# A half slot for the fifteenth expert slot of a top-1 mixture of experts

## The chip, the cores and the metric

The kernel runs on one core of a Trainium2 chip. The metric is device time in microseconds (us) of one execution, as the median of several runs. TensorE multiplies (PE in the views, PEld its weight loads), VectorE (DVE), ScalarE (ACT) and GpSimd (POOL) work element by element, and SyncE (SP) issues most of the transfers. PE writes into PSUM, from where ACT and DVE take the results.

## The reference, cut to what matters

```python
attn = sigmoid(q @ k.T / sqrt(64) - log(448)) @ v      # 4 batches, 12 heads, 448 tokens, heads of 64
x    = attn as (1792 tokens, 768)
e    = argmax(x @ w_gate, axis=1)                      # 8 experts, one per token
g    = softmax(x @ w_gate)[token, e]
x    = g * (relu(x @ w1[e]) @ w2[e])                   # w1: 768 x 1024, w2: 1024 x 768
h    = relu(x @ w_in)                                  # 768 x 2048
out  = (h * h) @ w_out                                 # 2048 x 768
```

With the inputs of the reference, worked out from its code, the eight experts get 25, 19, 434, 5, 260, 235, 456 and 358 tokens.

## The kernel before, in words

The kernel has three stages: attention with the gate's logits, the experts, and the two dense layers at the end. Its order is written out by hand; each engine takes its instructions in that order, and so does each queue of transfers.

**Numbers in two parts.** A product of two f32 numbers is made from parts that TensorE takes at a faster rate: a high part (ACT copies it, f32 to f32r) and a low part (DVE subtracts the high part from the number). `split_w` does both for a chunk of weights. A product then needs three passes over the weights: high by high, low by high, high by low. `passes` issues them.

**Slots.** A slot is 128 rows of one expert. The rows of a slot are gathered from `x_d` by an indirect transfer (`gather`), transposed and split (`xtrans`), multiplied by w1 in four chunks (`up(c)`, c = 0 to 3, three passes of three matmuls over 512 columns each), transposed (`htrans`), multiplied by w2 in four chunks (`down(c)`, c = 4 to 7, three passes of four matmuls over 384 columns each), scaled by the gate (`fin`) and written to `y_d`. Slots 0 and 1 take rows of the expert with the most tokens among the first twelve blocks of tokens, before all tokens are routed. The other slots are laid out over the experts in order. While slot s runs, the weights of slot s+1 are split chunk by chunk (`next_chunk`, `split_m`) and those of slot s+2 are loaded; a slot from the third on loads only if its expert differs from that of the slot before (`regd`).

**Quarter slots.** The last rows of an expert, if they are 1 to 32, go to one of four quarter slots, which use f32 weights directly and run a piece at a time between the chunks of slots 3 to 12. Their rows are copied to their place in `y_d` at the end of the first layer (`quarter_rows`).

**How many.** `NTL + 1` = 15 slots always run. Further ones stand in a conditional block (`tc.If(more < NT)`), which runs only if the rows need it. With the tokens above, slots 0 and 1 take 256 rows of expert 6, four experts use a quarter slot, and the rest needs 13 slots: 15 in all. Expert 2, with 434 tokens, takes four of them, the last one with 50 rows.

**Routing on DVE.** `slots` works out how many rows each expert gets in slots, `late_places` the place of each token, `late_picks` and `spots` the one-hot tables from which TensorE picks the rows of the slots (`pick_rows`, line 227). `slots` comes in slot 0 after the second chunk, `late_places` and the tables at the end of slot 0, `pick_rows` in slot 1 between the second and third chunk. `quarters` works out the quarter slots in slot 2, and `gates` after it fills the gate table `gts`, which ACT needs for the first result of slot 2 (`fin(6)`).

**The last slot.** In slot 14 no weights of a further slot are split. Between its chunks 0 to 3 the first four tiles of `y_d` are transposed for the dense layers (`trans_y`, line 721). Each uses the two PSUM tiles px0 and px1, which ACT (line 726) and DVE (line 727) empty. After chunks 4 and 5 the first weights of the dense layers are split (`stage`). Then comes the conditional block (line 1071) and the first dense layer (`layer1`, lines 1245 to 1247).

## Time and profile before

| | before |
|---|---|
| median of 3 runs | 929.45 us (929.14 to 930.36) |
| the profiled execution | 928.85 us |
| its span | 927.4 us |
| PE busy | 917.4 us (99%) |
| PEld busy | 771.8 us (83%) |
| DVE busy | 692.6 us (75%) |
| ACT busy | 567.5 us (61%) |
| POOL busy | 101.0 us (11%) |
| mean granted clock | 0.998 |

The span is the part of the profiled execution that the hardware recorded; 1.45 us of its time lie around it. The time of an instruction runs from its start to its modelled end, and matmuls overlap: what a row of matmuls costs is read from the starts of the rows that follow it, not from its length.

### The profile page before, as it was taken

The numbers are of one execution on the slowest core, as the hardware profiler recorded it, in microseconds if no ns is written. First come the engines' busy times: TensorE is split into PE (matmuls) and PEld (weight loads), VectorE is DVE, ScalarE is ACT, GpSimd is POOL, SyncE is SP. The second block draws the span as 40 slices with busy tenths as digits, with TensorE's granted clock in tenths as the row PEclk, the third lists the DMA queues.
The fourth block names the chain that finished last, engine by engine and source line by source line (L and its number), as shares of the span: only waits on it lengthen the run. The fifth ranks groups of instructions, "written<-read, shape, count | busy, mean of one in ns | idle before, by whom it ended". The sixth has DMA issues, their size and how long they took to land. (4 is left out here: it accounts for less than half of the span.)

```text
span 927.4 us, 15244 instructions
## 1 busy us (share of the span) xinstructions
PE 917.4 (99%) x5803; PEld 771.8 (83%) x5803; DVE 692.6 (75%) x849; ACT 567.5 (61%) x711; POOL 101.0 (11%) x139
## 2 busy tenths in 40 slices
PE   9999999999999999999999999999999999999997
PEld 4555555589888888889998888889999999999997
DVE  3888886599887776877866998748878766569863
ACT  5767665768777867767764455455544466666541
POOL 1000001110411110101001222110000210000002
PEclk9999999999999999999999999999999999999999
DMA  8798977672687969693445988564333355456312
GB/s 297 262 369 323 335 230 243 239 290 73 245 290 280 354 242 360 238 403 138 164 183 187 364 298 287 193 237 154 100 105 119 125 179 174 140 177 238 127 35 102
DMA packets 63986, 206.37 MB, mean 223 GB/s; under 512 B 9330, under 2 KB 29138, under 8 KB 62754
## 3 DMA queue, kind: packets, MB, share of 16 engines
q1 hardware_dynamic: 43570, 159.85, 49.4%
q0 software_dynamic: 9040, 39.73, 11.2%
q10 hardware_dynamic: 11296, 5.75, 2.2%
q8 instruction: 47, 0.77, 0.3%
q14 instruction: 33, 0.27, 0.1%
HBM read 210.40 MB, written 45.63 MB: 276 GB/s over the span
## 5 line engine op out<-in xcount | busy, mean ns | idle before, releaser
L501 DVE TENSOR_TENSOR wl<-raw,wh 128x1536 fp32r<-128x1536 f32 x109 | 190.0, 1758 | 55.1 <-ACT wh L500 51.9
L500 ACT ACTIVATE wh<-raw 128x1536 fp32r<-128x1536 f32 x109 | 160.0, 1482 | 0.4 <-ACT xn L444 0.4
L398 ACT ACTIVATE a<-sc,bias_s 128x896 f32<-128x896 f32 x96 | 82.6, 912 | 55.0 <-PE sc L394 55.0
L1426 PE MATMUL pq<-wrh,sh 128*128 128x384 f32 x264 | 89.0, 337 | 0.0
L1428 PE MATMUL pq<-wrh,sl 128*128 128x384 f32 x264 | 88.8, 336 | 0.0
L1427 PE MATMUL pq<-wrl,sh 128*128 128x384 f32 x264 | 88.7, 336 | 0.0
L501 DVE TENSOR_TENSOR wrl<-raw,wrh 128x1536 fp32r<-128x1536 f32 x25 | 43.8, 1756 | 22.3 <-ACT wrh L500 21.6
L500 ACT ACTIVATE wrh<-raw 128x1536 fp32r<-128x1536 f32 x25 | 37.0, 1483 | 38.1 <-PE pq L1428 38.1
L404 PE MATMUL po<-a,qkv 128*64 128x448 f32 x288 | 59.6, 548 | 0.0
L764 PE MATMUL py<-wh,hh 128*128 128x384 f32 x240 | 55.4, 352 | 0.0
L1272 DVE TENSOR_TENSOR sl<-h,sh 128x1024 fp32r<-128x1024 f32 (+1 forms) x47 | 51.6, 1111 | 4.2 <-ACT sh L1271 4.2
L764 PE MATMUL ph<-wh,xh 128*128 128x512 f32 x180 | 53.4, 405 | 0.0
L764 PE MATMUL ph<-wl,xh 128*128 128x512 f32 x180 | 52.9, 402 | 0.0
L764 PE MATMUL py<-wh,hl 128*128 128x384 f32 x240 | 51.8, 337 | 0.0
L764 PE MATMUL ph<-wh,xl 128*128 128x512 f32 x180 | 51.6, 395 | 0.0
L764 PE MATMUL py<-wl,hh 128*128 128x384 f32 x240 | 51.6, 336 | 0.0
L1428 PEld LDWEIGHTS pq<-wrh,sl 128*128 128x128 f32 x264 | 49.5, 188 | 0.3 <-DVE sl L1272 0.3
L1427 PEld LDWEIGHTS pq<-wrl,sh 128*128 128x128 f32 x264 | 49.5, 188 | 0.0
L1426 PEld LDWEIGHTS pq<-wrh,sh 128*128 128x128 f32 x264 | 49.5, 188 | 0.0
L1271 ACT ACTIVATE sh<-h 128x1024 fp32r<-128x1024 f32 (+1 forms) x47 | 44.5, 962 | 7.6 <-PE pq L1427 6.7
L404 PEld LDWEIGHTS po<-a,qkv 128*64 128x64 f32 x288 | 18.4, 136 | 32.7 <-issue 30.0
L1251 ACT ACTIVATE r<-pp 128x512 f32<-128x512 f32 x32 | 19.1, 598 | 43.0 <-PE pp L1247 42.9
(447 smaller groups left out, 2156.9 us busy)
## 6 DMA issues: line engine op xcount, KB each, us to landing
raw<-in_wm SPq DMA_DIRECT2D x110, 768.0 KB
qraw<-in_wm SPq DMA_DIRECT2D x32, 768.0 KB
raw<-t_d SPq DMA_DIRECT2D x28, 768.0 KB
cs<-in_w SPq DMA_DIRECT2D x9, 1536.0 KB
qkv<-in_qk SPq DMA_DIRECT2D x23, 480.0 KB
whc<-in_w SPq DMA_DIRECT2D x14, 768.0 KB
qkv<-in_v SPq DMA_DIRECT2D x24, 256.0 KB
w_d<-cd POOLq DMA_DIRECT2D x8, 768.0 KB, 8.3
```

Source lines behind the costliest of these rows:

```text
L398: nc.scalar.activation(a[:, :n], ps[:, :n, :S], AF.Sigmoid, bias=bias_s, scale=1.0 / math.sqrt(D))
L404: nc.tensor.matmul(po[64 * h:64 * h + 64, :S], vr[:, 128 * c + 64 * h:128 * c + 64 * h + 64], a[:, h], start=(c == 0), stop=False, skip_gr ...
L500: nc.scalar.activation(h, src, AF.Copy)
L501: nc.vector.tensor_tensor(l, src, f32(h), op=ALU.subtract)
L764: nc.tensor.matmul(ps, left(i, q), right(j, q), start=first and a == 0 and q == 0, stop=last and a == 2 and q == n - 1)
L1251: nc.scalar.activation(r[:, :N], pp[:, :N], AF.Relu)
L1271: nc.scalar.activation(sh[:, :2 * N], src, AF.Copy)
L1272: V.tensor_tensor(sl[:, :2 * N], src, f32(sh[:, :2 * N]), op=ALU.subtract)
L1426: nc.tensor.matmul(po[p][:, :DH], lh, wc[:, w0:w0 + DH], start=(q == 0 and kk == 0 and o in (0, 2, 5)), stop=False, **fl)
L1427: nc.tensor.matmul(po[p][:, :DH], lh, wcl[:, w0:w0 + DH], start=False, stop=False, **fl)
L1428: nc.tensor.matmul(po[p][:, :DH], ll, wc[:, w0:w0 + DH], start=False, stop=(q == 3 and kk == 1), **fl)
```

## The change

The base has 14 slots and a half slot. One expert whose last rows are 33 to 64 gives them to the half slot (the first such expert; here expert 2 with its 50 rows). The half slot gathers 64 rows; `xtrans` puts their high parts into columns 0 to 63 and their low parts into columns 64 to 127 of one operand. `up` and `down` of `make_half` run two passes over each chunk (the operand by the high weights, by the low weights). The result has 128 rows: rows 0 to 63 from the high parts, rows 64 to 127 from the low parts; the two belong together. For the hidden layer the sum is made by the transposition: instead of a transposition against the identity, `htrans` multiplies by `fold`, two identities of 64 below one another, in f32, and the ReLU comes after it. The final 128 rows go to `yh_d`; in the first dense layer they are read back as two tiles of 64 rows (`half_rows`), added on DVE and written to their place in `y_d` ahead of the quarter rows. The weights of the half slot are loaded in any case. The conditional block begins one slot earlier.

Routing gets more work: six more DVE instructions in `slots`, two more in `late_places`, eight more in `quarters`, and tables of 25 instead of 24 columns. `gates` issues two more transfers on POOL.

```diff
-LC = LSLOT + NQ
+LC = LSLOT + 1 + NQ
+HM = 64
+QC = NSLOT + 1
+NMAIN = NTL
-NBASE = NTL + 1
+NBASE = NMAIN + 1
...
+    fold = const.tile([128, HM], F32, name="fold")
+    nc.gpsimd.tensor_tensor(fold, ident[:, :HM], ident[:, HM:], op=ALU.add)
...
         V.tensor_tensor(sa[:, 0, 1:], full, t30, op=ALU.add)
+        V.tensor_scalar(t30, pn, 63.5 - HM, TWO30, op0=ALU.add, op1=ALU.add)
+        V.scalar_tensor_tensor(half, t30, -TWO30, full, op0=ALU.add, op1=ALU.subtract)
+        V.tensor_tensor(half, half, cand, op=ALU.subtract)
+        V.tensor_tensor_scan(hs, seg[:, 0, 1:E + 1], half, 0.0, op0=ALU.mult, op1=ALU.add)
+        V.scalar_tensor_tensor(half, hs, -128.0, half, op0=ALU.is_ge, op1=ALU.mult)
+        V.tensor_tensor(sa[:, 0, 1:], sa[:, 0, 1:], half, op=ALU.add)
...
-        V.scalar_tensor_tensor(dlt, qs[:, :E], -128.0 * LSLOT, sx[:, 0, 1:], op0=ALU.add, op1=ALU.add)
+        V.scalar_tensor_tensor(dlt, half, 0.0, qs[:, :E], op0=ALU.is_equal, op1=ALU.mult)
+        V.scalar_tensor_tensor(dlt, dlt, -128.0 * (LSLOT + 1), sx[:, 0, 1:], op0=ALU.add, op1=ALU.add)
+        V.tensor_tensor(dlt, dlt, half, op=ALU.subtract)
...
-                nc.tensor.transpose(pt[:, j - j0, :], xg[:, j * 128:(j + 1) * 128], ident)
-            nc.scalar.activation(xh[:, j0:j0 + n], pt[:, :n], AF.Copy)
-            nc.vector.tensor_tensor(xl[:, j0:j0 + n], pt[:, :n], f32(xh[:, j0:j0 + n]), op=ALU.subtract)
+                nc.tensor.transpose(pt[:, j - j0, :w], xg[:w, j * 128:(j + 1) * 128], ident[:w, :w])
+            nc.scalar.activation(xh[:, j0:j0 + n, :w], pt[:, :n, :w], AF.Copy)
+            low = xl[:, j0:j0 + n] if w == 128 else xh[:, j0:j0 + n, w:]
+            nc.vector.tensor_tensor(low, pt[:, :n, :w], f32(xh[:, j0:j0 + n, :w]), op=ALU.subtract)
...
+        def make_half(s, xc):
...
+            def htrans(i):
+                pt = ps_ht.tile([128, 4, 128], F32, tag="pht", name=f"pht_{s}_{i}")
+                for f in range(4):
+                    nc.tensor.matmul(pt[:, f, :HM], hr[i][:, f * 128:(f + 1) * 128], fold, start=True, stop=True, skip_group_check=True)
+                hi, lo = (hc[:, 4 * i:4 * i + 4, HM * k:HM * k + HM] for k in range(2))
+                nc.scalar.activation(hi, pt[:, :, :HM], AF.Relu)
+                nc.vector.scalar_tensor_tensor(lo, pt[:, :, :HM], 0.0, f32(hi), op0=ALU.max, op1=ALU.subtract)
+
+            def both(out, first, last, steps, left, right, turn=None):
+                for a in range(2):
+                    for q in range(steps):
+                        nc.tensor.matmul(out, left(q), right(a, q), start=first and a == 0 and q == 0,
+                                         stop=last and a == 1 and q == steps - 1)
+                    if a == 0 and turn:
+                        turn()
+
+            def up(c):
+                i = c // 2
+                if c % 2 == 0:
+                    ps[i] = ps_h.tile([128, 512], F32, tag=f"ph{i}", name=f"ph_{s}_{i}")
+                both(ps[i], c % 2 == 0, c % 2 == 1, 3, lambda q: xc[:, 3 * (c % 2) + q, :],
+                     lambda a, q: (mh[c], ml[c])[a][:, q * 512:q * 512 + 512], (lambda: htrans(0)) if c == 2 else None)
+                if c % 2 == 1:
+                    hr[i] = mp.tile([128, 512], F32, tag="hr", name=f"hr_{s}_{i}", bufs=1)
+                    nc.scalar.activation(hr[i], ps[i], AF.Copy)
+
+            def down(c):
+                fg, dh = (c - 4) // 2, c % 2
+                if fg == 0:
+                    ps[2 + dh] = ps_y.tile([128, 512], F32, tag=f"py{dh}", name=f"py_{s}_{dh}")
+                both(ps[2 + dh][:, :384], fg == 0, fg == 1, 4, lambda q: hc[:, 4 * fg + q, :],
+                     lambda a, q: (mh[c], ml[c])[a][:, q * 384:(q + 1) * 384])
+                if c == 4:
+                    htrans(1)
...
+            V.tensor_scalar(t30, hs, 0.0, None, op0=ALU.is_ge)
+            V.tensor_reduce(out=rq_h, in_=t30, op=ALU.add, axis=AX.X)
+            V.tensor_scalar(ctl[:, 0, NSLOT:QC], rq_h, float(E - 1), None, op0=ALU.min)
-            V.tensor_tensor(rows_q, sa[:, 2, 1:], sa[:, 1, 1:], op=ALU.subtract)
+            V.tensor_tensor(t30, sa[:, 2, 1:], sa[:, 1, 1:], op=ALU.subtract)
+            V.scalar_tensor_tensor(rows_q, half, 0.0, t30, op0=ALU.is_equal, op1=ALU.mult)
+            V.tensor_tensor(t30, t30, rows_q, op=ALU.subtract)
+            V.tensor_reduce(out=rq_h, in_=t30, op=ALU.add, axis=AX.X)
+            V.tensor_tensor(rq_h, rq_h, sx[:, 1, E:E + 1], op=ALU.add)
+            V.tensor_scalar(ctl[:, 2, NSLOT:QC], sx[:, 1, E:E + 1], float(NT), None, op0=ALU.min)
...
+            for j in range(2):
+                nc.gpsimd.dma_start(out=gh[HM * j:HM * j + HM], in_=gts[:HM, NSLOT:QC])
...
+    def half_rows(n):
+        if n == 7:
+            for k in range(2):
+                parts_h.append(xgp.tile([128, DM + 2], F32, tag="xg", name=f"hp_{k}", bufs=2)[:HM, :DM + 1])
+                nc.sync.dma_start(out=parts_h[k], in_=yh_d[HM * k:HM * k + HM, :DM + 1])
+        elif n == 11:
+            V.tensor_tensor(parts_h[0][:, :DM], parts_h[0][:, :DM], parts_h[1][:, :DM], op=ALU.add)
+
     def quarter_rows():
+        hrow = nc.gpsimd.value_load(ctl[0:1, 2, NSLOT:QC], min_val=0, max_val=NT)
+        nc.gpsimd.dma_start(out=y_d[ds(hrow, HM), :DM + 1], in_=parts_h[0])
...
             combine()
+            half_rows(sum(seen.values()))
```

## Rows read from the trace of the kernel before

**Rows 1.** Windows: stretch, length, busy of each engine (instructions), clock, DMA share, GB/s.

```profile
230.00:449.00 219.00, 218.76 (x1955) 192.86 (x1954) 169.14 (x138) 161.93 (x181) 32.20 (x29) 1.00 0.74 270
...
488.00:620.00 132.00, 131.59 (x586) 107.98 (x587) 104.32 (x155) 65.63 (x98) 25.85 (x40) 1.00 0.77 268
```

**Rows 2.** Timeline of PE in slot 14: start, length, line, tiles, count, [idle before].

```profile
467.23 0.86 PE L764 MATMUL ph<-wh,xh 128*128 128x512 f32 x3
467.92 0.86 PE L764 MATMUL ph<-wh,xl 128*128 128x512 f32 x3
...
472.66 0.95 PE L764 MATMUL ph<-wh,xh 128*128 128x512 f32 x3
...
474.14 0.60 PE L788 MATMUL pht<-ident,hr 128*128 128x128 f32 x4
474.50 0.94 PE L764 MATMUL ph<-wl,xh 128*128 128x512 f32 x3
...
486.14 0.86 PE L764 MATMUL py<-wl,hh 128*128 128x384 f32 x4
486.83 0.86 PE L764 MATMUL py<-wh,hl 128*128 128x384 f32 x4
488.41 0.50 PE L1245 MATMUL pp<-yt,wrh 128*128 128x512 f32 x1 [0.72 <-ACTq L1071]
```

**Rows 3.** Timeline of DVE at the beginning of slot 14.

```profile
469.42 1.76 DVE L501 TENSOR_TENSOR wl<-raw,wh 128x1536 fp32r<-128x1536 f32 x1 [0.31 <-ACT wh L500]
...
471.28 1.02 DVE L727 TENSOR_TENSOR yt<-pyt,yt 128x384 fp32r<-128x384 f32 x2
```

**Rows 4.** Timeline of PE ahead of slot 0.

```profile
178.01 0.95 PE L436 MATMUL lgT<-pick,ls 96*112 96x8 f32 x8
178.82 0.94 PE L764 MATMUL ph<-wh,xh 128*128 128x512 f32 x3
```

**Rows 5.** Timeline of DVE in slots 0 and 1.

```profile
186.80 0.17 DVE L260 SCALAR_TENSOR_TENSOR t<-qs,cand 128x8 f32<-128x8 f32 x1
187.00 0.17 DVE L261 TENSOR_TENSOR sa<-full,t 128x8 f32<-128x8 f32 x1
...
188.27 0.68 DVE L790 TENSOR_TENSOR hl<-pht,hh 128x512 fp32r<-128x512 f32 x1
...
199.22 2.69 DVE L223 TENSOR_SCALAR big<-iot,plf 112x128 f16<-112x128 f16 x16
...
203.88 3.43 DVE L501 TENSOR_TENSOR wl<-raw,wh 128x1536 fp32r<-128x1536 f32 x2 [1.39 <-ACT wh L500]
```

**Rows 6.** Timelines of PE (first two) and ACT in slots 0 and 1.

```profile
189.37 0.86 PE L764 MATMUL py<-wh,hl 128*128 128x384 f32 x4
...
202.04 0.94 PE L764 MATMUL ph<-wh,xh 128*128 128x512 f32 x3
...
201.88 0.60 ACT L802 ACTIVATE hr<-ph 128x512 f32<-128x512 f32 x1 [3.67 <-PE ph L764]
```

**Rows 7.** Timelines of DVE (first two), ACT and PE in slots 2 and 3.

```profile
231.02 0.20 DVE L941 TENSOR_TENSOR cmq<-srow,qs 128x32 f32<-128x32 f32 x1
...
232.42 0.23 DVE L948 TENSOR_SCALAR ctl<-rq__140,sx 128x4 int32<-128x4 f32 x1
...
235.94 0.58 ACT L818 ACTIVATE y<-py,gts 128x384 f32<-128x384 f32 x1 [3.29 <-DVE gts L957]
...
241.87 0.66 PE L788 MATMUL pht<-ident,hr 128*128 128x128 f32 x4 [0.24 <-ACT hr L802]
```

**Rows 8.** Windows, as in rows 1: about slots 9 and 12.

```profile
358.00:379.00 21.00, 21.00 (x157) 18.73 (x156) 16.73 (x14) 16.14 (x20) 1.83 (x2) 1.00 0.96 394
...
428.00:449.00 21.00, 21.00 (x225) 18.57 (x224) 16.84 (x13) 15.09 (x17) 1.10 (x1) 1.00 0.05 21
```

**Rows 9.** Timelines of POOL and SP around the end of the first dense layer.

```profile
622.87 0.50 POOL L1221 DMA_DIRECT2D y_d<-yq_d  x1 [2.79 <-DMA y_d<-yq_d]
...
635.60 1.91 SPq L1127 DMA_DIRECT2D yp<-y_d  x4
```

## The prediction

> **What bounds the kernel now.** I read the windows first: through the slots and through the first dense layer PE is busy for all but 0.2 and 0.4 us of the stretch, with the other engines well below it [rows 1]. So PE sets the time, and an edit counts by what it takes out of PE's order or by the wait that it puts into it. A microsecond lost on PE is not won back later, since PE has no idle time to give.

> What a pass costs has to be read from the timeline, by starts. Three matmuls over 512 columns are shown with 0.86 us, but the next pass starts 0.69 to 0.70 us later, and it is the same for four matmuls over 384 columns [rows 2]. Matmuls overlap, so the lengths overstate a pass by a fifth.

> **Does the change do what it says?** By the token counts worked out from the reference, the 15 slots of before become 14 and a half slot holding 50 rows of expert 2. The conditional block stays empty. So PE loses work.

> **Slot 14, the gain.** Each of eight chunks loses one of three passes: 4 x 0.70 + 4 x 0.70 = 5.6 us. Two things are taken back.

> First, a wait at the second `trans_y`. In slot 14 DVE is still at the last split of slot 13's list: it starts at 469.42 behind ACT and leads straight to the emptying of the first `trans_y` tiles at 471.28, two operations ending at 471.84 (half of their time plus) and 472.30 [rows 3]. The second `trans_y` needs these tiles. Before, PE ends it at 472.66 [rows 2] and hardly waits. With one pass less in each of two chunks PE arrives 1.4 us earlier, but what DVE does hangs on the end of slot 13, which doesn't move. PE then ends the second `trans_y` at the same 472.65: the 1.4 us of chunks 0 and 1 become a wait. After that two passes (1.4 us), six transpositions and, once, `fold` lie between a `trans_y` and the next, and emptying two tiles takes DVE 1.02 us [rows 3] behind ACT; I expect no more than 0.3 us of waits there, and put none into the sum.

> Second, `fold` against the transposition. A transposition of four blocks takes 0.36 us (474.14 to 474.50 [rows 2]). `fold` is an ordinary f32 product, and the trace has one near it in size: `token_logits` makes four f32 matmuls of 8 columns with 96 by 112 weights. The view counts eight instructions, so each f32 matmul is two, and they take 0.81 us, 178.01 to 178.82 [rows 4]. `fold` has 64 columns, few enough that loading weights should still rule: 0.8 us for four, 0.45 more than now, twice: 0.9 us. The low bound is the transposition itself (nothing lost), the high one two f32r-like steps per matmul at 0.70 / 4 = 0.175 us: 8 x 0.175 = 1.4 us, 1.05 more each, 2.1 us together. I take 0.9, as rows 4 have the same data type and also load weights for each matmul.

> [...]

> The gain is 5.6 - 1.4 - 0.9 = 3.3 us; by the bounds 2.1 to 4.2, and 1.4 more if the wait at `trans_y` doesn't come. ACT's and DVE's halves of `xtrans` and `htrans` get shorter (64 columns for 128), but nothing waits for them. The gap of 0.72 us to layer 1, where PE waits for ACT past the conditional block, stays [rows 2].

> **Routing, the loss.** Short DVE operations that follow one another start 0.20 us apart, though they are 8 elements wide (186.80, 187.00 [rows 5]). `slots` gets six in a chain: 1.2 us. `late_places` gets two more in a chain: 0.4 us. The wider tables are 4% more of two operations of half a microsecond, under 0.05 us.

> From `slots` to the end of `spots` the timeline marks no idle time on DVE, so all of it moves. The first to feel it is the low part of slot 0's hidden layer (`hl`, 188.27, ending at 188.95 [rows 5]): 1.2 later it ends at 190.15, and the third pass of chunk 4, at 189.37 [rows 6], waits 0.8 us. Then `spots`, which ended at 199.22 + 2.69 = 201.91 [rows 5] with PE going on at 202.04 [rows 6], ends at 203.5, and PE goes on at 203.65: 1.6 us lost in all, the 0.8 included.

> In slot 1 DVE starts again at 203.88, after an idle 1.39 us that ACT ended [rows 5], and ACT had waited for PE's second chunk (201.88 [rows 6]). That chunk stands ahead of the wait for `spots`, so it is only 0.8 late. From there DVE has no idle time until `gts`. In slot 2 `quarters` now has 16 short operations for 8, which took 231.02 to 232.65 [rows 7]: five of the new ones in chains at 0.2, three beside others at 0.1, 1.3 us. So `gts` is 0.8 + 1.3 = 2.1 us late. ACT waits for `gts` already, 3.29 us at the first result of slot 2, everything on ACT stands behind it, and the next thing that PE needs from ACT is the hidden layer of slot 3, where PE waits 0.24 us now (241.87 [rows 7]). That comes 2.1 to 2.2 late; PE, 1.6 late by itself, waits for the rest. The loss is 2.2 us in all. Bounds: 1.6 if the wait in slot 3 is covered, 3.0 if DVE is fully 1.6 late in slot 1 as well.

> [...]

> **What costs nothing.** `fold` is built on POOL before the first attention unit, which doesn't wait for it. The half slot's weights (8 chunks of 768 KB, 6.3 MB) are loaded in any case; before, slot 14 had the expert of slot 13 and loaded nothing, and the stretch of slot 12 in which they now come uses 0.05 of the transfer engines. About slot 9, weights and quarter loads together ran at 394 GB/s with PE busy throughout [rows 8]. The two parts of the half slot are added in the first dense layer, one DVE operation of about 1 us where DVE has 28 us of 132 idle [rows 1]. The half's rows go out on POOL ahead of the four quarter writes, which follow one another at some 3 us; the last is issued at 622.87, and SP reads `y_d` again only at 635.60 [rows 9], so one more such step is covered. If that cover went, the second block's first tiles would be late. The two transfers more in `gates` are POOL's alone.

> **The sum.** -3.3 + 2.2 = -1.1 us. The profiled execution, 928.85 us (span 927.4 and 1.45 around it), would take 927.75. The median of the runs shown is 0.6 higher, 929.45, and becomes 928.4. About 0.2%, 1.86 us, is what a measurement can tell from no change (below 927.6 or above 931.3).

> **Rivals.**
> 1. *The routing is absorbed.* If the added operations overlap, or PE's order has slack that the view doesn't mark, the loss falls to 0 to 0.8 us: 926.2 to 927.0, faster. For it: short operations that don't depend on one another start closer. Against it: `spots` and PE's next pass stand 0.13 us apart, and the chains are chains. 17%.
> 2. *No wait at the second `trans_y`.* Then the gain is 4.7, and the time 927.0. It needs DVE 1.2 us earlier; the half operand's smaller `xtrans` pieces come ahead of ACT's last splits, but these wait for PE's end of slot 13. 8%.
> 3. *The load isn't hidden: slower.* Slot 14's weights are split in slot 13, and their buffers are free only after the split in slot 12, one slot before (slot 14 itself lasts 21 us to layer 1 [rows 2]). 6.3 MB in 21 us need 300 GB/s. It decides when the rate falls below that: at 250 GB/s the last chunk is 4 us late, and the time 932.4. Against it are the 394 GB/s [rows 8]. 6%.
> 4. *The half slot doesn't replace a slot*, and a fifteenth runs in the conditional block, about 20 us more: 949. Only if the tokens differ from the counts. 2%.

> My forecast, a small gain, has 60%, with its own range of 927.2 (4.2 - 1.6 less, and 0.3 for the likelier inner ends) to 929.7; another 7% I leave to small sums that end near no change. From these: faster 5 + 17 + 8 = 30%, within 0.2% 55 + 7 = 62%, slower 8%. The range, 926.4 to 930.6, takes in the sum of the bounds (-2.6 and +0.9 us) and rivals 1 and 2 in part.

> **What the profile after would show.** Fourteen slots and a half one: 24 passes less 8 in the last. PE idle at the second `trans_y`, about 1.2 us, ended by DVE's line 727. `fold` as sixteen f32 instructions of PE, 0.8 us for each group of eight. In slot 0 a wait of PE for `hl` of 0.8 us, in slot 1 another 0.8 us at `pick_rows`, ended by `spots`; in slot 3 ACT's wait for `gts` longer, and PE's wait at the transposition 0.5 us longer. The start of layer 1, 488.41 now, near 487.3, and the same distance from there to the end. I am wrong if PE's order through slots 0 to 3 ends as early as before, if `fold` takes the time of a transposition, or if DVE's split at the start of slot 14 ends earlier.

## The result and the profile after

The changed kernel takes 934.72 us (median of 5 runs, 933.32 to 935.53) against 929.45 us (928.77 to 930.36): ratio 1.0057, 95% interval 1.0045 to 1.0068. It is 5.3 us slower; 928.4 us had been forecast. The profiled execution takes 934.75 us, with a span of 933.3.

PE is still the bound. Its timeline through the places that the forecast names:

```profile
190.52 0.79 PE L783 MATMUL py<-wh,hl 128*128 128x384 f32 x3 [0.70 <-DVE hl L809]
...
203.97 0.48 PE L783 MATMUL ph<-wh,xh 128*128 128x512 f32 x1
...
244.36 0.33 PE L807 MATMUL pht<-ident,hr 128*128 128x128 f32 x1 [0.84 <-ACT hr L821]
...
469.38 0.86 PE L862 MATMUL ph<-wh,xh 128*128 128x512 f32 x3
...
474.04 1.01 PE L738 MATMUL pyt<-ident,yr 128*128 128x128 f32 x6 [1.05 <-DVE yt L744]
474.81 0.95 PE L862 MATMUL ph<-wh,xh 128*128 128x512 f32 x3
475.59 1.00 PE L854 MATMUL pht<-fold,hr 128*128 128x64 f32 x8
476.40 0.48 PE L862 MATMUL ph<-wl,xh 128*128 128x512 f32 x1
...
485.67 0.86 PE L862 MATMUL py<-wl,hc 128*128 128x384 f32 x4
489.41 0.50 PE L1338 MATMUL pp<-yt,wrh 128*128 128x512 f32 x1 [2.88 <-ACTq L1152]
```

Read against [rows 2, 6 and 7], start by start: slot 0's low half waits where it did not (0.70 us); slot 1 goes on 1.93 us later; slot 3's transposes are 2.49 late; the last slot starts 2.15 late (469.38 for 467.23), but its last pass is 1.16 early (485.67 for 486.83), so that slot became 3.31 us shorter. Then layer 1 starts 1.00 us late. From the last pass to layer 1 it is now 3.74 us, for 1.58 before. The conditional block, whose body does not run, stands between them. Its own instructions, in the view of its line (first before, then after; engine's queue, instruction, min/median/max in ns, first start):

```profile
L1071 PEldq COMPARE_BRANCH  x1: 3502/3502/3502, 484.4 to 484.4; - x1
L1071 ACTq COMPARE_BRANCH  x1: 54/54/54, 487.7 to 487.7; - x1
...
L1071 ACTq EVENT_SEMAPHORE  x1: 17/17/17, 488.3 to 488.3; - x1
```

```profile
L1152 PEldq COMPARE_BRANCH  x1: 5257/5257/5257, 483.3 to 483.3; - x1
L1152 ACTq COMPARE_BRANCH  x1: 54/54/54, 486.6 to 486.6; - x1
...
L1152 ACTq EVENT_SEMAPHORE  x1: 17/17/17, 489.3 to 489.3; - x1
```

PE and ACT each have their own branch (COMPARE_BRANCH), which jumps over the body; ACT's EVENT_SEMAPHORE is its first instruction behind the jump. Two things are longer. PE's branch (in PEld's queue) took 3.50 us and takes 5.26. ACT's branch itself takes 54 ns in both, but ACT's next event came 0.6 us after it and now comes 2.7 us after it; layer 1 waits for that event. The windows behind it (clock in the third column from the end), after and then before:

```profile
490.00:492.00 2.00, 2.00 (x7) 1.57 (x6) 1.05 (x1) 0.92 (x1) 0.00 (x0) 0.59 0.00 0
492.00:496.00 4.00, 4.00 (x15) 3.17 (x15) 3.10 (x4) 0.55 (x1) 0.00 (x0) 0.78 0.00 0
```

```profile
490.00:492.00 2.00, 2.00 (x11) 1.63 (x10) 2.00 (x2) 0.00 (x0) 0.00 (x0) 1.00 0.18 68
492.00:496.00 4.00, 4.00 (x19) 3.34 (x18) 3.11 (x5) 2.02 (x3) 0.00 (x0) 1.00 0.00 0
```

After the idle 2.88 us some of layer 1's first matmuls ran at a lower granted clock (0.50 of full speed from 490.5 to 493 us, starts 0.427 us apart instead of 0.233): 7 matmuls for 11 between 490 and 492 us. From the first to the 18th matmul record of layer 1 it is 5.61 us for 4.01, so 1.6 us; by the 18th the clock is back (1.00 from 494 us on).

The rest lies where no wait has changed (one of 0.4 us, at `pi`, stands in both kernels). The dense layers run in two blocks of tokens: the first block writes `pp` (first layer) and then `pq` (second layer), the second block writes `pi` (first layer) and then `pq` again. Five marks on PE's timeline cut the remaining run into four stretches, one for each layer of each block: the 18th matmul record of layer 1, the first `pq`, the first `pi`, the last `pi` and the last `pq`. After, and then before:

```profile
495.02 0.40 PE L1340 MATMUL pp<-yt,wrl 128*128 128x512 f32 x1
...
627.68 0.33 PE L1520 MATMUL pq<-rh,sh 128*128 128x384 f32 x1
...
748.92 0.70 PE L1401 MATMUL pi<-xw,wrh 128*128 128x384 f32 x3
...
837.98 0.33 PE L1401 MATMUL pi<-x7k,rl 128*128 128x384 f32 x1
...
926.81 0.34 PE L1522 MATMUL pq<-wrh,sl 128*128 128x384 f32 x1
```

```profile
492.42 0.39 PE L1247 MATMUL pp<-yt,wrl 128*128 128x512 f32 x1
...
623.35 0.33 PE L1426 MATMUL pq<-rh,sh 128*128 128x384 f32 x1
...
744.57 0.68 PE L1308 MATMUL pi<-xw,wrh 128*128 128x384 f32 x3
...
833.01 0.33 PE L1308 MATMUL pi<-x7k,rl 128*128 128x384 f32 x1
...
920.88 0.34 PE L1428 MATMUL pq<-wrh,sl 128*128 128x384 f32 x1
```

The stretches between them, in us:

```
                    to pq   to pi  to last pi  to last pq
before             130.93  121.22     88.44       87.87
after              132.66  121.24     89.06       88.83
before_placed      132.64  121.27     89.06       88.82
after_home         130.88  121.23     88.41       87.86
before_shift32     131.53  121.28     89.03       88.84
after_shift32      132.54  121.59     88.85       88.66
after_placed       131.65  121.62     88.82       88.67
before_eight       130.87  121.21     88.43       87.88
after_no_cond      132.64  121.24     89.02       88.84
after_seven_late   133.38  121.25     89.04       88.84
after_best         132.41  121.22     88.41       87.89
after_final        136.69  120.89     88.42       87.87
```

The kernels below the second line are experiments. So the loss of 5.9 us at the last matmul is made of 0.3 (attention, which ended between 178.6 and 180.0 in the profiles of kernels that share its code), 1.85 (slots 0 to 13, with the added routing), -3.31 (last slot), 2.16 (block), 1.6 (clock), 1.73 and 0.02 (first block of tokens, first and second layer) and 0.62 and 0.96 (second block, the same).

### The profile page after: what moved, and what is told of

It is laid out like the page before. It is cut to its first block, busy times and chain, and to the rows that moved or that the text cites. A ratio compares the mean times of both kernels' runs of the same rounds, so it can differ in the third digit from the quotient of the medians.

```text
span 933.3 us, 15231 instructions
## 1 busy us (share of the span) xinstructions
PE 918.9 (98%) x5783; PEld 770.0 (83%) x5783; DVE 695.4 (75%) x866; ACT 567.1 (61%) x711; POOL 106.0 (11%) x143
## 5 line engine op out<-in xcount | busy, mean ns | idle before, releaser
L783 PE MATMUL py<-wh,hh 128*128 128x384 f32 x224 | 51.6, 352 | 0.0
L783 PE MATMUL ph<-wh,xh 128*128 128x512 f32 x168 | 49.6, 403 | 0.0
L783 PE MATMUL ph<-wl,xh 128*128 128x512 f32 x168 | 49.4, 402 | 0.0
L783 PE MATMUL py<-wh,hl 128*128 128x384 f32 x224 | 48.2, 337 | 0.7 <-DVE hl L809 0.7
L783 PE MATMUL ph<-wh,xl 128*128 128x512 f32 x168 | 48.3, 395 | 0.0
L783 PE MATMUL py<-wl,hh 128*128 128x384 f32 x224 | 48.1, 336 | 0.0
```

What stands on the lines that cost most here:

```text
L783: nc.tensor.matmul(ps, left(i, q), right(j, q), start=first and a == 0 and q == 0, stop=last and a == 2 and q == n - 1)
```

## Experiments

Theories: (1) the block's gap and the low clock behind it, (2) the addresses that the change's longer tables shift, (3) what makes the block slow on ACT and PE, (4) VectorE work placed ahead of something that is waited for.

**Without the conditional block** (the overflow slots are left out), in both kernels.

```diff
-        with tc.If(more < NT):
-            for s in range(NMAIN, NSLOT):
...
```

> The changed kernel with its conditional block left out (the eight overflow slots, which the inputs here don't need). Theory 1: of the 5.3 us lost, 2.2 are PE's longer branch at the block (5.26 us against 3.50, ending later than the down pass by 2.88 us) and some 1.6 us the half clock of the 9 matmuls after that idle time. Then the gap to layer 1 goes from 2.88 us to under 0.3, the granted clock of 488:500 stays at 1.00 (0.86 in the changed kernel), and the time is 934.7 - 2.9 - 1.6 = 930.2 us (929.5 to 931). Rival: the gap only shows what ACT or the DMA queues are late with at that point; then some other wait of 2 to 3 us stands in the same place and the time stays within 1 us of 934.7.

> The kernel before with its conditional block left out (seven overflow slots, not needed here). Theory 1: PE's gap of 0.72 us to layer 1 goes, and nothing else: 928.7 us (928.2 to 929.2). Rival, the block costs more than its gap, since registers are loaded and engines meet there: 926 to 928. Beside the run without the block of the changed kernel it gives the difference of the two without the boundary: forecast there, 2.2 (routing) - 3.3 (last slot) = -1.1 us; if the changed kernel's slower matmul pace in layer 1 belongs to the change, +1 us or more instead.

Measured: 930.42 us and 928.08 us, ratios to before 1.0011 (1.0002 to 1.0020) and 0.9991 (0.9982 to 1.0000). The gap went and the clock stayed (1.00 from 488 to 496 us in both), 4.3 us less than the changed kernel, as theory 1 had it. The kernel before came out 0.1 us under its range. But with no block in either, the changed kernel is still 2.3 us slower where -1.1 was forecast, and the table still has the 3.3 us in the dense layers. The block is one of two causes.

**What makes the block slow.** Four loads behind it, one slot in it, seven slots in it, and eight in the kernel before:

```diff
 after_late_fetch
-                fetch_half(PRE, 0)
-                fetch_half(PRE, 1)
+    # (behind the block, with the two load_y of yns)
 after_short_body
-            for s in range(NMAIN, NSLOT):
+            for s in range(NSLOT - 1, NSLOT):
 after_seven
-            for s in range(NMAIN, NSLOT):
+            for s in range(NMAIN + 1, NSLOT):
 before_eight
-            for s in range(NBASE, NSLOT):
+            for s in range(NBASE - 1, NSLOT):
```

> The changed kernel with four loads (two halves of 768 KB of layer 2's first weights, two row tiles of 385 KB) issued after the conditional block instead of in the last slot. Theory 1a: PE's branch takes long because the instructions at its target are fetched behind these loads, so its end follows the first load's issue by some 10 us in both kernels (477.52 to 487.9; 478.72 to 488.56). Then the branch takes under 2 us, the gap of 2.88 us goes, the clock stays up and the time is 930 to 931 us. Rival 1b: the branch is long because of what it jumps over (eight slots against seven); then the branch stays at 5 us, the gap at 2.9 and the time at 934.7 or above, since the loads are later.

> The changed kernel with one overflow slot in the conditional block instead of eight (the inputs here need none). Rival 1b (the length of what is jumped over sets the branch): the branch falls from 5.3 us to about 1, the gap of 2.88 us goes, 930 to 931 us. Theory 1a (the fetch waits behind the loads): branch, gap and time stay as in the changed kernel, 934.7 us (934 to 935.5).

> The kernel before with eight slots in the conditional block instead of seven (slot 14 once more; none is executed with these inputs). Theory 3: ACT's first instruction after the jump comes 0.6 us after its branch with seven slots (and with one, in the changed kernel) and 2.7 us after it with eight, so the eighth slot alone makes the gap to layer 1 grow from 0.72 to some 2.8 us, and the clock falls after it: 929.4 + 2.1 + 1.6 = 933.1 us (931 to 933.5). Rival 3b: what is late on ACT comes from the half slot in front of it (its loads, its shorter passes); then 929.4 us.

> The changed kernel with seven slots in the conditional block instead of eight (slot 14 is left out of the overflow; not needed with these inputs). Theory 3: the gap to layer 1 falls from 2.88 us to about 0.7, no half clock, 931.1 us as with one slot (930.5 to 932). Rival 3b: 934.7 us with the gap of 2.9. A share of the length (one eighth less to jump over) would give 934.3.

Measured: late loads 934.44 us (ratio 1.0058, 1.0045 to 1.0072), one slot 931.14 (1.0021, 1.0012 to 1.0030), eight slots before 934.52 (1.0054, 1.0041 to 1.0068), seven slots after 932.97 (1.0039, 1.0025 to 1.0053). The times alone would mislead; the block's instructions say more. Late loads: PE's branch fell to 3.33 us (theory 1a had expected under 2), but ACT's event still came 2.8 us after its branch, and the gap stayed 2.91 us:

```profile
L1148 PEldq COMPARE_BRANCH  x1: 3332/3332/3332, 483.7 to 483.7; - x1
...
L1148 ACTq COMPARE_BRANCH  x1: 54/54/54, 487.0 to 487.0; - x1
...
L1148 ACTq EVENT_SEMAPHORE  x1: 17/17/17, 489.8 to 489.8; - x1
```

Seven slots: ACT's event came 0.6 us after its branch, but PE's branch took 5.53 us, and the gap was 2.5 us with PE as its own releaser:

```profile
L1152 PEldq COMPARE_BRANCH  x1: 5532/5532/5532, 483.6 to 483.6; - x1
...
L1152 ACTq COMPARE_BRANCH  x1: 54/54/54, 486.8 to 486.8; - x1
L1152 ACTq EVENT_SEMAPHORE  x1: 17/17/17, 487.4 to 487.4; - x1
```

So two delays lie side by side, and taking away one shows the other. Eight slots before:

```profile
L1071 ACTq COMPARE_BRANCH  x1: 54/54/54, 488.9 to 488.9; - x1
...
L1071 ACTq EVENT_SEMAPHORE  x1: 17/17/17, 491.9 to 491.9; - x1
```

One more slot in a block that is never executed made the kernel before 5.1 us slower, 1 us more than the expected range allowed: ACT's event came 3.0 us after its branch, the gap was 3.2 us, and the low clock followed. In the profiled execution the gap is 2.4 us of the loss and the clock 1.6; another 1.2 us lies ahead of slot 0, in attention, which this edit doesn't touch. One slot:

```profile
L1152 PEldq COMPARE_BRANCH  x1: 352/352/352, 483.4 to 483.4; - x1
...
L1152 ACTq COMPARE_BRANCH  x1: 54/54/54, 486.6 to 486.6; - x1
L1152 ACTq EVENT_SEMAPHORE  x1: 17/17/17, 487.3 to 487.3; - x1
```

**Both delays taken away:** seven slots and the late loads.

> The changed kernel with seven slots in the conditional block and its four loads issued after the block. Theory 3, put together: PE's branch is a fetch that the loads delay (5.5 us with them, 3.3 without), ACT's is late by the eighth slot (2.7 us, else 0.6); with both taken away the gap to layer 1 is 0.7 to 1.2 us and the clock stays: 934.7 - 1.9 - 1.6 = 931.2 us (930.5 to 932). Rival: with ACT early, PE's own branch still ends at 488.5 or later whatever is loaded: gap 2.5, 933 us as with seven slots alone.

Measured: 932.19 us (1.0030, 1.0018 to 1.0042). The gap is 0.72 us and the clock stays, as expected, but the time is 1 us higher than expected: the late loads cost 0.7 us in layer 1, the first stretch of the table.

**Length or landing place.** The kernel before, still with seven slots, and 41 ACT instructions of one column spread over slots 5 to 11:

```diff
+                if 4 < s < 12 and 4 * s + c < 46:
+                    for _ in range(2 if 4 * s + c < 35 else 1):
+                        nc.scalar.activation(warm, bias_s, AF.Copy)
```

> The kernel before with 41 very short ACT instructions (one element per partition, on a scratch tile) spread over slots 5 to 11, 28 more in ACT's program all told up to the branch, since some semaphore instructions fall away: with seven slots jumped over (182 instructions) the jump lands at instruction 831 of ACT's program, against 803 before and 829 with eight slots. Theory 3d (the landing place counts: it must lie in a stretch of the program that is already fetched): ACT's first event 2.7 us after its branch, gap to layer 1 some 2.8 us, half clock after it, 933 to 934.6 us. Rival 3e (the length of the jump counts): 0.6 us after its branch, gap 0.72, 929.4 to 930 us.

Measured: 932.9 us (1.0035, 1.0021 to 1.0049), just under the expected range. Slots 5 to 14 kept their pace; the block did not:

```profile
L1074 ACTq COMPARE_BRANCH  x1: 54/54/54, 488.0 to 488.0; - x1
...
L1074 ACTq EVENT_SEMAPHORE  x1: 17/17/17, 490.8 to 490.8; - x1
```

2.8 us with the same seven slots: the landing place counts, not the length of the jump. This run moves the branch itself by the same 28 instructions, but in before_eight the branch stays where it was; the later landing place is what the two share. (The instruction numbers 803, 829 and 831 are counted in the compiled program, from its first instruction to the branch and over the body.)

**Addresses.** First 32 bytes in front of the tiles of layers 1 and 2, in both kernels; then three unused tiles that put the tiles of the kernel before, but for some small tables, where the change puts them, and three that bring the changed kernel's residues back; then the changed kernel with `fold` and the row-number table in the pool that closes before layer 1, so that layers 1 and 2 have exactly the addresses of before.

```diff
 before_shift32, after_shift32
+    nc.gpsimd.memset(dp.tile([128, 8], F32, name="pad"), 0.0)
 before_placed (72, 40, 8), after_placed (8, 8, 8)
+    nc.gpsimd.memset(const.tile([128, 72], F32, name="pad0"), 0.0)
+    nc.gpsimd.memset(rt([128, 40], "pad1"), 0.0)
+        nc.gpsimd.memset(mp.tile([128, 8], F32, name="pad2", bufs=1), 0.0)
 after_home
-    fold = const.tile([128, HM], F32, name="fold")
-    tok = const.tile([128, NCOL], U32, name="tok")
+    tok = rq.tile([128, NCOL], U32, name="tok")
+    fold = rq.tile([128, HM], F32, name="fold")
```

> The kernel before with 32 bytes in front of the tiles of layers 1 and 2 (weight ring, activations, evictions), so that their SBUF addresses change from 32 to 0 modulo 64, as the change's longer tables make them. Theory 2: of what the changed kernel lost, 1.8 us between the first matmul of layer 1 and the first of layer 2, and 1.6 us after the last pi tile, come from these addresses (both show in the runs without the conditional block too, where nothing waits). Then this kernel takes 929.4 + 3.4 = 932.8 us (931.5 to 933.5). Rival 2b: the pace belongs to something else in the changed kernel (its half_rows loads, its DMA traffic, the order of its evictions); then 929.4 us.

> The changed kernel with the same 32 bytes, which brings the tiles of layers 1 and 2 back to 32 modulo 64. Theory 2: 934.7 - 3.4 = 931.3 us (930.5 to 932.5), the first matmul of layer 1 to the first of layer 2 134.9 us plus 1.6 for the low clock, and last pi to last pq 87.9 us as before instead of 88.8. Rival 2b: 934.7 us.

> The kernel before with three unused tiles (288, 160 and 32 bytes) that put every tile at the SBUF address it has in the changed kernel; nothing else is changed. Theory 2: addresses alone slow layers 1 and 2 as in the changed kernel: from the 18th matmul of layer 1 to layer 2 132.6 us instead of 130.9, first to last pi 89.0 instead of 88.4, from there to the last pq 88.8 instead of 87.9, so 929.4 + 3.3 = 932.7 us (932 to 933.5). The shift of the tiles of layers 1 and 2 alone gave 0.6, 0.6 and 1.0 of it, so the rest (1.1 us in layer 1) must come from the row tiles and raw weights that lie before them. Rival 2b: that rest comes from work the changed kernel adds in layer 1 (loads and a sum for the half slot's rows); then 931.5 us as with the shift alone.

> The changed kernel with three unused tiles of 32 bytes, which bring all tiles to the residues modulo 64 that they have in the kernel before. Theory 2: 934.7 - 3.3 = 931.4 us (930.8 to 932.3), with 130.9, 88.4 and 87.9 us in the three stretches. Rival 2b: 933.2 us, with 132 in the first.

> The changed kernel with the fold matrix and the row-number table in the pool that is closed before layer 1, and a spare tile of 96 bytes, so that the row tiles, raw weights and all tiles of layers 1 and 2 lie at exactly the addresses of the kernel before. Theory 2 (the addresses, not their residue modulo 64): 130.9, 88.4 and 87.9 us in the three stretches, 934.7 - 3.3 = 931.4 us (930.8 to 932.2). Rival 2b (work that the changed kernel adds): 132.6, 89.0 and 88.8 us, 934.7 us.

Measured: before_shift32 931.44 us (1.0024, 1.0015 to 1.0033), after_shift32 934.04 (1.0051, 1.0037 to 1.0065), before_placed 932.23 (1.0032, 1.0020 to 1.0044), after_placed 935.08 (1.0060, 1.0046 to 1.0074), after_home 933.20 (1.0047, 1.0033 to 1.0061). The table settles theory 2 in both directions: before_placed, which adds nothing but unused tiles, has the changed kernel's stretches to 0.03 us, and after_home, which leaves the change's work in, has those of before. The residue modulo 64 does not settle it: after_placed got back 1.0 of 1.7 us in the first stretch and 0.4 of 1.6 in the last two, and lost 0.4 in the second; after_shift32, the farthest from its expectation, got back 0.1 in the first, where before_shift32 had lost 0.6. The five marks on PE's timeline, of before_placed and then of after_home:

```profile
491.94 0.40 PE L1250 MATMUL pp<-yt,wrl 128*128 128x512 f32 x1
...
624.58 0.33 PE L1429 MATMUL pq<-rh,sh 128*128 128x384 f32 x1
...
745.85 0.70 PE L1311 MATMUL pi<-xw,wrh 128*128 128x384 f32 x3
...
834.91 0.33 PE L1311 MATMUL pi<-x7k,rl 128*128 128x384 f32 x1
...
923.73 0.34 PE L1431 MATMUL pq<-wrh,sl 128*128 128x384 f32 x1
```

```profile
496.71 0.39 PE L1342 MATMUL pp<-yt,wrl 128*128 128x512 f32 x1
...
627.59 0.33 PE L1522 MATMUL pq<-rh,sh 128*128 128x384 f32 x1
...
748.82 0.68 PE L1403 MATMUL pi<-xw,wrh 128*128 128x384 f32 x3
...
837.23 0.33 PE L1403 MATMUL pi<-x7k,rl 128*128 128x384 f32 x1
...
925.09 0.34 PE L1524 MATMUL pq<-wrh,sl 128*128 128x384 f32 x1
```

after_home also lost something: from the start of slot 4 to that of slot 14 it took 210.3 us, for 209.3 before and 209.0 in the changed kernel, because its slot tiles lie elsewhere again. That, and not its layers, is most of why it gained 1.5 us and not the 3.3 expected. PE waits for nothing in these ten slots either, and the time goes with the layout there too: 208.9 us in before_placed, 210.3 in after_best and after_spread, which have the addresses of after_home. So the changed kernel's layout won it 0.3 us in the slots.

**Routing alone, and its order.** Sixteen short instructions on a scratch tile in the kernel before; and the changed kernel with `quarters` behind the gate copies.

```diff
 before_routing
+        for _ in range(6):      # slots; 2 in late_places, 8 in quarters
+            V.tensor_tensor(t30, t30, full, op=ALU.add)
 after_order
-                    quarters()
                     q_gather(0)
...
                     gates()
+                    quarters()
```

> The kernel before with sixteen short VectorE instructions (6 where the slots are worked out, 2 where the positions are, 8 in front of the quarters' tables) on a scratch tile, as many as the change adds there. The step of the forecast on routing: 0.8 us of wait at slot 0's low half, 1.6 in all by slot 1's row picks, 2.2 by slot 3: 929.4 + 2.2 = 931.6 us (930.8 to 932.2). Rival: VectorE's backlog is absorbed before slot 3, 929.4 to 930.2.

> The changed kernel with the tables of the quarters and the half slot (27 short VectorE instructions) worked out after the gate copies of slot 2 instead of before them. Theory 4 (the added VectorE work costs where it stands before something that ACT and then PE wait for): PE's wait at slot 3's transposes (0.84 us) goes, 934.7 - 0.7 = 934.0 us (933.6 to 934.4). Rival: the wait is for something else that is late, 934.7.

Measured: before_routing 931.71 us (1.0027, 1.0016 to 1.0037), some 2.4 us over before for 2.2 expected. Its waits on PE:

```profile
PE pht L792 <- ACT hr L806: 1.1, 1, 1.1
PE pp L1251 <- ACTq L1077: 0.7, 1, 0.7
PE py L768 <- DVE hl L794: 0.6, 1, 0.6
```

after_order took 932.78 us (1.0036, 1.0022 to 1.0050). The wait in slot 3 went, and the last slot starts 0.55 us earlier (468.83), although attention ended 0.5 later: some 1.0 us for 0.7 expected. The rest of the 1.9 us doesn't come from this edit. Three executions lie at 932.0 to 932.8 us with a mean clock of 0.998, two at 934.4 and 935.4 with 0.996 and 0.995; the profile, of the last, has the low clock behind the gap. That it stayed away in the three is an inference from their mean clock.

**Whole kernels with the causes taken away.** after_best: addresses of after_home, order of after_order, the two halves late, and two ReLUs and two output copies per overflow slot on VectorE. after_spread: besides, the last slot's transposes after chunks 0, 2, 4 and 5. after_final: only `fold` and one small table moved, all four loads late, and half of the overflow slots' weight splits begun on GpSimd.

> The changed kernel whole, with the addresses of after_home, the quarters' tables after the gate copies, the two halves of layer 2's first weights loaded after the conditional block, and in the block's eight slots two ReLUs and two output copies each on VectorE instead of ACT (159 ACT instructions to jump over instead of 208; seven slots had 182). If the three causes add up: 934.7 - 3.3 (addresses) - 0.7 (order) - 2.2 (gap) - 1.6 (clock) + 0.4 (later loads) = 927.3 us (926.6 to 928.5), that is faster than before by 2 us, 1.1 of it forecast for the change itself. Rival 3c (ACT's late instruction depends on where its code lies and not on how many are jumped over): the gap of 2.8 us and the half clock stay, 930.5 us or more.

> The kernel of after_best with the last slot's four row-tile transposes after its first and third up blocks and its first two down blocks, instead of after each of the four up blocks. If PE's wait of 1.05 us at the second transposes comes from VectorE's backlog there, it goes and the time is 1.0 us under after_best; the rival is that layer 1 then waits for the last transposed tile by as much or more: the same time or up to 1 us over it.

> The changed kernel whole: fold matrix and one small table in the pool that is closed before layer 1, so that layers 1 and 2 have the addresses of the kernel before and the slots those of the changed kernel; the quarters' tables after the gate copies; all four loads after the conditional block, row tiles first; and in the block's eight slots half of the weight splits' first step on GpSimd instead of ACT (146 ACT instructions there). 934.7 - 3.3 (addresses) - 0.7 (order) - 2.2 (gap) - 1.6 (clock) + 0.5 (later loads) = 927.4 us (926.8 to 928.6): faster than before by 0.1 to 0.3%. If the causes don't add up, 929.4 or more.

Measured: 929.67 us (1.0006, 0.9997 to 1.0015), 929.48 (1.0002, 0.9993 to 1.0011) and 932.47 (1.0032, 1.0020 to 1.0044). None is faster than before. In all three ACT's event came 0.5 to 0.6 us after its branch (146 and 159 ACT instructions to jump over), no clock was lost at the block (1.00 from 480 to 500 us), and the second block of tokens had the stretches of before. after_best lost 1.5 us in the first stretch (one wait of 1.3 us for a row tile) where 0.4 was allowed for the late loads, and 1.3 in slots 4 to 13, which its expectation had left out. after_final lost 5.8 us in the first stretch: 3.9 in the waits below, and some 1.7 to a granted clock of 0.63 in the 4 us from 508 and 0.94 in the next 4. Waits on PE in after_final:

```profile
PE pyt L738 <- DMA yn<-y_d: 2.8, 2, 2.5
PE pp L1341 <- ACT r L1347: 1.1, 1, 1.1
```

The row tiles that layer 1 transposes second are queued behind the late halves. In after_spread the last slot became 1.2 us shorter than in after_best (15.2 us from its start to its last pass, for 16.4), but the gap, which DVE's queue ends in both, grew by 0.5 and the medians differ by 0.2: most of the wait was moved, as the rival had it.

## Why the prediction was wrong

**The failed step** is "The gap of 0.72 us to layer 1, where PE waits for ACT past the conditional block, stays [rows 2]", and with it "the same distance from there to the end". The forecast took the block, which doesn't execute, as a fixed wait. The change makes its body eight slots for seven, and that moved the place where ACT's jump lands: 2.7 us to the next event instead of 0.6, shown by before_eight and, with the length unchanged, by before_more_act. PE's branch became longer too (5.26 for 3.50), with the four loads nearer in front of it; after_late_fetch took 1.9 us off it by moving them. In sum 2.2 us of gap and, in the profiled execution, 1.6 us of low clock behind it: 3.8 us.

The profile's transfers show what lies inside PE's branch. In every profiled kernel with seven or eight slots in the block, one instruction transfer of 16 KB (queue q8) starts there, and the branch ends 2.3 to 2.8 us after that start. With one slot none starts there, and the branch takes 0.35 us. Before, the transfer starts 1.0 us after the branch does (485.44 for 484.4); in the changed kernel it starts 2.8 us after it (486.10 for 483.3), and until then, while the four loads land, the DMA share is 0.96; in after_late_fetch it is 1.0 us again. That PE's branch waits for this transfer is inferred from these times. The other queue with instruction transfers, q14, moved two of 8 KB between 485 and 488.5 us before (485.90 and 488.30) and three in the changed kernel (486.69 to 487.51), and the profile doesn't say for which engine: that ACT waits for one, too, is inferred from the landing place.

Over the profiled kernels, PE's branch takes 3.3 to 5.5 us over seven or eight slots, 0.35 over one; ACT's next event comes 2.7 to 3.0 us after its branch when the landing place is at instruction 829 or later, 0.5 to 0.7 when it is at 804 or earlier. Theory 3d's reason for it, that the landing place must lie in a stretch of the program that is already fetched, was the author's estimate: no run shows what is fetched when.

**The missing term** is the addresses: 3.3 us on the dense layers. The forecast costed the added tables by the work on them, not by where they push the tiles behind them (288 bytes). Shown by before_placed and after_home. The loss is spread over the matmuls: from 497 to 625 us those of `pp` start 229.6 ns apart on the mean before and 229.5 in after_home, but 232.6 in the changed kernel and in before_placed. What it is in an address that counts stays open. Block and clock (3.8), addresses (3.3 in the dense layers, less 0.3 in the slots) and attention (0.3) are, to 0.1 us, the 7.0 us between the 1.1 us forecast as gain and the 5.9 lost in the profile.

**The terms that were summed hold.** Slot: forecast -3.3, measured -3.31, with its parts: PE goes on after the second `trans_y` 5.43 us after the slot's start, as before (474.81 for 472.66), behind a wait of 1.05 us (1.2 named in the forecast); there is no other wait in the slot, and `fold` takes 0.81 us per group (475.59 to 476.40) where 0.8 was taken from the f32 product; PEld is busy through the whole 0.81 us in both. For scale, in attention of the kernel before an f32 product over 448 columns takes 0.84 us (149.02 to 149.86), one pass over the split parts 0.20 (148.00 to 148.20). Routing: 0.8 forecast at slot 0's low half, 0.70 measured; 1.6 by slot 1, 1.64 (1.93 less the 0.29 with which attention ended later), where 0.68 of it shows not as one wait but in `pick_rows`, whose sixteen short matmuls fill 1.10 us (202.87 to 203.97) for 0.42 before; 2.2 by slot 3, 2.20, of which the layout wins 0.3 back by slot 14; alone, 2.4. The loads for the half slot, the sum of its parts and its writes cost nothing: no wait of PE from slot 0 on names a transfer. With the block taken from both kernels the difference is +2.3 us, which is -1.1 and the 3.3 of the addresses to 0.1 us. One number of the forecast does not follow from its bounds: the upper end of its own range, 929.7, would be 930.05 by them (929.45 + 0.9 - 0.3); nothing else hangs on it.

**The rivals.** None of the four came. No run shows the loss of 0 to 0.8 us on which the first stood: it was 2.20 us by slot 3. The one on the slower side, loads that are not hidden, has no wait to show. The mechanism that decided was not among them, though rows 2 showed its wait.

## What to carry to other kernels

A conditional block that never runs was not free and not fixed here (without it the kernel before was 1.3 us shorter, the changed one 4.3): look at its line in every engine's queue, and when a change adds code in front of it or in it, count that as a change of its cost, with the idle time and the clock behind it. When a change adds or widens a constant table, put it where it moves no tile of a later stage, or compare with a kernel that has only the shift; in after_home such a move won 3.3 us in the dense layers and cost 1.3 in the slots. And when two delays end at the same point, removing either can show little of its worth (0.3 us for the late loads, 1.8 for the eighth slot, 2.5 for both): read each engine's own event.
